# Gated mix of segmented linear-memory attention and a ReGLU feed-forward: value visits in pairs, a ring of eleven exponential tiles, and a new written-out order

## The chip, the cores and the metric

The kernel runs on one core of one Trainium2 chip. Its time is the device time of one execution in microseconds (us), lower is better; three runs of the kernel before have a median of 267.24 us. Engines are named as in the profile: PE is TensorE (matmuls; PEld its weight loads), DVE is VectorE, ACT is ScalarE, POOL is GpSimd, SP is SyncE, which here issues DMAs.

## The reference

Input is x of 2048 tokens by 512. The output is g * a + (1 - g) * b with a gate g per token, an attention branch a and a feed-forward branch b. Cut to what is computed:

```python
g = sigmoid((x * gate_w).sum(-1))                    # per token
# attention branch: 32 heads of 16, 4 segments of 512 tokens
for s in range(4):
    p     = softmax(q_s @ k_s.T / 4 + causal_mask)   # within the segment
    a_dot = p @ v_s
    a_mem = (phi(q_s) @ M) / (phi(q_s) @ z + 1e-6)   # phi(t) = t + 1 if t > 0 else exp(t)
    o_s   = gb * a_mem + (1 - gb) * a_dot            # gb = sigmoid(beta), per head
    M, z  = M + phi(k_s).T @ v_s, z + phi(k_s).sum()
a = concat(o_s) @ wo
# feed-forward branch
b = (relu(x @ W_gate) * (x @ W_up)) @ W_down         # 512 -> 1792 -> 512
```

## The kernel before

Everything stays in SBUF after the first loads. The work is cut into four segments of 512 tokens, and in each segment into four units c of 128 channels, which are eight heads. Units are counted through: segment 0 has units 0 to 3, segment 3 has 12 to 15 in that count of sixteen, and a unit pair is two units that follow each other.

Each piece of work is a step with a name, a list of steps it comes after, and one function that emits its instructions (`Plan.add`, L123). The order is not searched for when the kernel is built: `ORDER` (L41 to L100) is a list of numbers, each one a step and the engine that runs it, and `lay_out` (L137) only puts the steps into their engines' queues in that order and hands out PSUM banks. So which engine evicts what, and what stands behind what on each queue (SP's too), is written out by hand. Every engine runs its queue strictly in order.

PSUM has eight banks. Four are one tile, `sp` (L241), for logits. The other four are `rb` (L242); a step that needs one takes it, and the step that reads it out gives it back.

The kinds of visit to TensorE that the change and the prediction speak of:

- *Ordinary visits* use the whole array: projections Q and K (L477) and V (L519; L502 in segment 0), gate and up (L894), down (L928) and the output projection (L941), retrievals from the memory (MR, L678). Each takes one `rb` bank. Evictions are on ScalarE or VectorE (L373 and L375; L906 and L908 for relu; L913 for the product).
- *Logits visits* (QK, L735) fill `sp`. They work on eight small tiles of the array at once, 4 x 2. Even heads use K itself, odd heads a copy in which the even heads' rows are zero (KTo, made by L490 or L492). Nine logits visits serve a unit pair. Each is followed by one exponential of 128 x 2048 on ScalarE (L746) into one of the E tiles, which form a ring of NE, and by masks on GpSimd (L756), one for each 64-row half of a diagonal block. There is one `sp`, so a logits visit waits for the exponential of the one before.
- *Value visits* (PV, L783), one for a unit, multiply the eight groups of a unit's E tiles with V. They work on tiles 2 x 4 and take two `rb` banks. Each bank is read by a transpose on VectorE (L801) into one of two tA tiles, and then by a chain of three operations (L806, L809, L812); the next transpose into the same tA tile waits for the chain's end. A transpose back (L828) and the memory's part (L834) follow.
- *Memory visits* (MZ, L632) work on tiles 1 x 4, one for a segment but the last.

The key blocks of a unit are packed into E tiles by `BINS`: a unit has eight blocks of 64 keys, block ck with 512 - 64 ck columns of queries. Tiles 0 to 3 of a pair hold the first unit's blocks as `BINS` lists them, tile 4 holds block 4 of both units, tiles 5 to 8 the second unit's.

```python
BINS = ((0,), (1, 7), (2, 6), (3, 5))                                  # L30
parts[w].append((5 * w + b, w, L - 64 * ck, ck, 64 * ck, at))          # L717
a = add(f"QK{seg}{c0}{f}", {"PE": 0.262}, qk, mode="rows", ... fills[-1:] ...)   # L739
b = add(f"EX{seg}{c0}{f}", {"ACT": 1.773}, ex,                         # L747
        after=[a] + readers.get(n - NE, []) + ([masks[n - NE]] if n >= NE else []), ...)
pp = a = add(f"PV{seg}{c}", {"PE": 1.02}, pv, mode="cols2",            # L788
             after=[masks[base + f] for f in need] + d["V"] + d["VS"], take=2, ...)
```

KTo and the tile of phi(Q) (pqT, L555, read by the retrievals) are there twice, one for even and one for odd segments.

In the order before, a value visit stands between ordinary and logits visits, one by one: the first unit's some way into its pair's nine logits visits or behind them, the second unit's later.

## Time and profile before

| what | value |
|---|---|
| median of three runs | 267.24 us (266.77 to 267.49) |
| span of the profiled execution | 265.0 us |
| logits visits, exponentials | 72, 135.1 us of ScalarE |
| masks | 256, 112.3 us of GpSimd |
| value visits | 16 |
| HBM read and written | 8.26 MB and 2.10 MB |

The profile gives the span of one execution, from its first instruction to its last; no time around the span is known for that execution, so it stands beside the median of the runs, which is 2.2 us above it. In rows of a group, after the bar, stand busy time in us, mean ns of one, and the idle time of the engine just before them with what ended most of it. In rows of the timeline stand start in us, duration in us, engine, line and operation. The durations of matmuls are modelled and overlap, so the starts are what is read. In rows of waits stand the waiting engine, tile and line, what it waited for, and then us in total, times and the longest.

### The profile page before, as it was taken

Reading aid. Unit: us, or ns where it says so; the run is one execution under the profiler, and the core shown is the slowest. Engines: PE = TensorE matmul, PEld = TensorE weight load, DVE = VectorE, ACT = ScalarE, POOL = GpSimd, SP = SyncE. Lnnn points to the kernel's source line nnn. Section 1 sums busy time; section 2 is a strip of 40 time slices with the busy share of each in tenths; the row PEclk is TensorE's granted clock in tenths of the full one; section 3 lists DMA queues with packets and bytes.
Section 4 is the critical chain, followed back from the end, with each engine's and each line's share of the span. In section 5 each row is a group of like instructions: output and inputs, shape, how many; then the busy total and the mean of one; then the engine's idle time right before and its main releaser. Section 6 shows DMA issues by size and latency. Waiting matters only on the chain.

```text
span 265.0 us, 7943 instructions
## 1 busy us (share of the span) xinstructions
PE 258.1 (97%) x3293; PEld 121.0 (46%) x3337; DVE 181.0 (68%) x449; ACT 189.7 (72%) x185; POOL 143.7 (54%) x328
## 2 busy tenths in 40 slices
PE   7999999999999999999999999999999999999995
PEld 5444443545444444434444445454544444444554
DVE  1589788897774538855896476688878367666911
ACT  3699799987868786887777686886766576767012
POOL 8038978782826641378758464366468156064010
DMA  6978680426501000030403110000023100031002
GB/s 197 314 166 264 149 288 3 71 74 89 79 4 37 25 2 2 20 82 1 104 2 82 25 42 2 0 4 2 2 61 87 42 20 2 0 81 23 0 2 79
DMA packets 33422, 16.77 MB, mean 63 GB/s; under 512 B 20074, under 2 KB 33386, under 8 KB 33386
## 3 DMA queue, kind: packets, MB, share of 16 engines
q1 hardware_dynamic: 33098, 16.00, 24.3%
q8 instruction: 26, 0.43, 0.7%
q10 hardware_dynamic: 288, 0.26, 0.3%
q14 instruction: 10, 0.08, 0.1%
HBM read 8.26 MB, written 2.10 MB: 39 GB/s over the span
## 4 chain that ended last, share of the span: by engine, by line
PE 94%; DMA 1%; DVE 1%; issue 1%; ACT 1%; SPq 0%
PE rb L894 36%; PE rb L928 17%; PE rb L477 11%; PE sp L735 9%; PE rb L783 7%; PE rb L941 5%; PE rb L519 4%; DMA wv_sb<-in_A_wv_dram 1%; PE rb L678 1%; PE rb L852 1%; PE rb L502 1%; DVE hT L913 1%; ACT E L746 1%; PE rb L632 1%; PE rb L860 0%
## 5 line engine op out<-in xcount | busy, mean ns | idle before, releaser
L746 ACT ACTIVATE E<-sp 128x2048 bf16<-128x2048 f32 x72 | 135.1, 1877 | 35.0 <-PE sp L735 32.8
L756 POOL TENSOR_SCALAR_AFFINE_SELECT E<-E 64x256 bf16<-64x256 bf16 x256 | 112.3, 438 | 82.2 <-ACT E L746 68.7
L894 PE MATMUL rb<-xT,wg_sb 128*128 128x512 bf16 x216 | 55.4, 380 | 0.4
L894 PE MATMUL rb<-xT,wu_sb 128*128 128x512 bf16 x208 | 54.9, 380 | 0.8
L913 DVE TENSOR_TENSOR hT<-rb,rg 128x512 bf16<-128x512 f32 x56 | 38.2, 686 | 20.1 <-PE rb L894 14.1
L928 PE MATMUL rb<-wd_sb,hT 128*128 128x512 bf16 x198 | 48.6, 380 | 0.8 <-issue 0.2
L894 PEld LDWEIGHTS <-wg_sb 128*128 128x128 bf16 x224 | 20.7, 98 | 24.8 <-issue 3.1
L894 PEld LDWEIGHTS <-wu_sb 128*128 128x128 bf16 x224 | 20.1, 98 | 23.5 <-issue 4.5
L735 PE MATMUL sp<-QT,KT 16*64 16x320 bf16 (+7 forms) x512 | 30.3, 295 | 0.0
L735 PE MATMUL sp<-QT,KTo 32*64 32x320 bf16 (+7 forms) x512 | 30.3, 295 | 0.0
L928 PEld LDWEIGHTS <-hT 128*128 128x128 bf16 x210 | 19.4, 98 | 23.8 <-issue 3.2
L801 DVE STREAM_TRANSPOSE tA<-rb 128x512 f32<-128x512 f32 x32 | 21.9, 700 | 12.0 <-PE rb L783 11.6
L906 ACT ACTIVATE rg<-rb 128x512 bf16<-128x512 f32 x36 | 21.3, 598 | 10.1 <-PE rb L894 7.1
L735 PEld LDWEIGHTS <-KT 16*64 16x64 bf16 x512 | 10.5, 102 | 27.5 <-issue 26.9
L908 DVE TENSOR_SCALAR rg<-rb 128x512 bf16<-128x512 f32 x20 | 13.8, 688 | 7.5 <-PE rb L894 7.3
L783 PE MATMUL rb<-E,Vs 64*32 64x448 bf16 (+7 forms) x512 | 18.8, 284 | 0.0
L783 PE MATMUL rb<-E,Vp 64*32 64x448 bf16 (+7 forms) x512 | 18.4, 284 | 0.0
L950 ACT ACTIVATE osb<-rb,ngcol 128x512 bf16<-128x512 f32 x8 | 5.5, 691 | 16.2 <-PE rb L941 16.2
L952 DVE TENSOR_SCALAR osb<-rb,ngcol 128x512 bf16<-128x512 f32 x7 | 5.2, 750 | 16.1 <-PE rb L941 15.9
L477 PE MATMUL rb<-xT,wq_sb 128*128 128x512 bf16 x63 | 16.1, 380 | 0.0
L812 DVE TENSOR_TENSOR o<-tA,co 128x256 bf16<-128x256 f32 x32 | 15.4, 493 | 0.2
L477 PE MATMUL rb<-xT,wk_sb 128*128 128x512 bf16 x59 | 15.4, 379 | 0.2
(97 smaller groups left out, 298.3 us busy)
## 6 DMA issues: line engine op xcount, KB each, us to landing
out_dram<-osb SPq DMA_DIRECT2D x15, 128.0 KB, 1.8
wd_sb<-in_B_W_down_dram SPq DMA_DIRECT2D x1, 1792.0 KB
wg_sb<-in_B_W_gate_dram SPq DMA_DIRECT2D x3, 512.0 KB, 6.3
wu_sb<-in_B_W_up_dram SPq DMA_DIRECT2D x3, 512.0 KB, 6.0
Vs<-Vp SPq DMA_DIRECT2D x8, 144.0 KB, 3.2
wk_sb<-in_A_wk_dram SPq DMA_DIRECT2D x2, 256.0 KB, 3.9
wq_sb<-in_A_wq_dram SPq DMA_DIRECT2D x2, 256.0 KB, 4.7
wo_sb<-in_A_wo_dram SPq DMA_DIRECT2D x1, 512.0 KB, 4.2
```

The source lines that it names most:

```text
L477: nc.tensor.matmul(rb[s.bank][:], lhsT=w[:, ci, c * P:(c + 1) * P], rhs=xT[i][:, ci, :], start=(ci == 0), stop=(ci == NC - 1))
L735: nc.tensor.matmul(sp[64 * h:64 * h + 64, j, off:off + m], lhsT=kt[32 * j:hi, c0 + w, 64 * ck:64 * ck + 64], rhs=QT[i][32 * j:hi, c0 + w, ...
L746: nc.scalar.activation(Er[n % NE][:], sp[:], ACT.Exp, scale=SCALE)
L756: nc.gpsimd.affine_select(out=v, in_=v, compare_op=ALU.is_ge, fill=0.0, base=0, pattern=[[0, 4], [1, 64]], channel_multiplier=-1)
L783: nc.tensor.matmul(rb[s.banks[h]][32 * j:32 * j + 32, q0:q0 + m], lhsT=v[64 * h:64 * h + 64, ck // 2, o:o + 32], rhs=Er[(base + f) % NE][6 ...
L801: nc.vector.transpose(tA[k].rearrange("p b w -> p (b w)"), rb[a.banks[r]][:])
L812: nc.vector.tensor_tensor(o16[u % 2][:, :, r, :], tA[k][:, :, 0:DH], cos[k][:, :, None].to_broadcast([P, NB, DH]), ALU.mult)
L894: nc.tensor.matmul(rb[s.bank][:], lhsT=w[:, ci, fv * P:(fv + 1) * P], rhs=xT[i][:, ci, :], start=(ci == 0), stop=(ci == NC - 1))
L906: nc.scalar.activation(rgb[k][:], rb[a.bank][:], ACT.Relu)
L908: nc.vector.tensor_scalar(rgb[k][:], rb[a.bank][:], 0.0, None, ALU.max)
L913: nc.vector.tensor_tensor(hT[:, fv, :], rb[a.bank][:], rgb[k][:], ALU.mult)
L928: nc.tensor.matmul(rb[b][:], lhsT=hT[:, fv, lc:lc + P], rhs=wd_sb[:, fv, :], start=(fv == 0), stop=False)
```

## The change

- Both value visits of a unit pair stand back to back on TensorE, between two logits visits or behind the last ordinary visit.
- The ring of E tiles has eleven instead of nine.
- KTo and pqT are there once; the KTo mask of a segment now also comes after the logits visits of the segment before, and phi(Q) after the retrievals of the segment before (until now, of the one before that).
- `BINS` puts block 0, the one with 512 columns and two masks, into the last tile of each unit and not into the first.
- `ORDER` is written anew for all engines: other places of steps, and other engines for some of those that two engines can run.

```diff
-NE = 9
+NE = 11
-BINS = ((0,), (1, 7), (2, 6), (3, 5))
+BINS = ((1, 7), (2, 6), (3, 5), (0,))
 ORDER = [
...
-    KTo = [sb([NC, L], BF16, f"KTo{i}") for i in range(2)]
-    pqT = [sb([NC, L], BF16, f"pqT{i}") for i in range(2)]
+    KTo = sb([NC, L], BF16, "KTo")
+    pqT = sb([NC, L], BF16, "pqT")
...
-            d["KO"].append(add(f"KO{seg}{c}", {"DVE": 0.27, "ACT": (0.62, 60.0)}, ko, after=[d["K"][c]], prio=want))
+            d["KO"].append(add(f"KO{seg}{c}", {"DVE": 0.27, "ACT": (0.62, 60.0)}, ko,
+                               after=[d["K"][c]] + (st[seg - 1]["qk"][c] if seg else []), prio=want))
...
                 d["PQ"].append(add(f"PQ{seg}{c}", {"DVE": dve(L)}, pq2,
-                                   after=[m] + (old["mr"] if old else []), prio=want))
+                                   after=[m] + st[seg - 1]["mr"], prio=want))
...
-                        kt = KTo[i] if h else KT[i]
+                        kt = KTo if h else KT[i]
```

The order on TensorE around the first value visits, by the steps' names (U, G gate and up, V, K, Q projections, D down; first digit the segment), before:

```
QK007 | V121 U0_3 | PV00 | QK008 | V130 G0_6 K13 G0_7 | QK020 ...
QK022 | MZ0 | G0_9 | PV01 | QK023 | V120 G0_13 U0_9 MR11 | QK024
```

and after:

```
QK008 | G0_8 Q12 U0_6 | QK020 | K13 G0_10 U0_10 | QK021 | PV00 PV01 | QK022 | V120 G0_11 G0_13 | QK023
```

Behind the pairs stand, in the new order: units 0-1, 2-3, 6-7 and 10-11 a logits visit; units 4-5, 12-13 and 14-15 a gate or up visit; units 8-9 a memory visit.

## The prediction

> **What bounds the kernel now.** I read the page's busy table and its chain first, then TensorE's own waits, then TensorE's timeline where it goes from one kind of work to another.

> ```profile
> span 265.0 us, 7943 instructions
> PE 258.1 (97%) x3293; PEld 121.0 (46%) x3337; DVE 181.0 (68%) x449; ACT 189.7 (72%) x185; POOL 143.7 (54%) x328
> ...
> PE 94%; DMA 1%; DVE 1%; issue 1%; ACT 1%; SPq 0%
> ```

> TensorE is busy 97% of the span and carries 94% of the chain that ended last. A busy TensorE is no proof that it never waits, since matmul ends are modelled. So the next view is what TensorE waited for:

> ```profile
> PE rb L380 <- DVE zeros L252: 1.0, 1, 1.0
> PE rb L502 <- DMA wv_sb<-in_A_wv_dram: 0.3, 1, 0.3
> PE rb L390 <- DMA xT<-in_A_x_dram: 0.3, 1, 0.3
> PE rb L928 <- issue: 0.2, 1, 0.2
> ```

> Except for 0.2 us these waits belong to the first loads. Between them and the end the next matmul always stands ready. So the time is the sum of what TensorE streams plus what it pays for changing its tiling. No other engine has anything to give unless it makes TensorE wait. The price of a change stands in the starts of the timeline:

> ```profile
> 41.25 1.03 PE L894 MATMUL rb<-xT,wg_sb 128*128 128x512 bf16 x4
> 42.11 1.03 PE L894 MATMUL rb<-xT,wu_sb 128*128 128x512 bf16 x4
> 43.07 0.21 PE L735 MATMUL sp<-QT,KT 16*64 16x64 bf16 x1
> ...
> 43.12 0.35 PE L735 MATMUL sp<-QT,KT 16*64 16x448 bf16 x1
> ...
> 43.43 0.82 PE L894 MATMUL rb<-xT,wu_sb 128*128 128x512 bf16 x3
> ```

> An ordinary visit of four matmuls follows its like after 42.11 - 41.25 = 0.86 us. The one ahead of a logits visit takes 43.07 - 42.11 = 0.96, so the change to another tiling costs 0.10. The logits visit lasts 43.43 - 43.07 = 0.36 with its own change back. A value visit:

> ```profile
> 88.30 0.21 PE L783 MATMUL rb<-E,Vs 64*32 64x64 bf16 x4
> ...
> 88.90 0.56 PE L783 MATMUL rb<-E,Vp 64*32 64x448 bf16 x8
> 89.09 0.39 PE L783 MATMUL rb<-E,Vs 64*32 64x512 bf16 x4
> ...
> 89.40 0.24 PE L735 MATMUL sp<-QT,KT 16*64 16x128 bf16 x1
> ```

> It lasts 1.10 us. Inside it, the group of 448 columns passes to the next group after 0.19 us, so the last one, of 512, would pass to another group of the same tiling after 0.19 x 512/448 = 0.22. It passes to the logits visit after 0.31, so leaving the tiling costs about 0.09 to 0.10.

> **The change, part by part.** I counted the tiling changes in the two orders of TensorE's instructions: 164 before, 151 after.

> *Entries.* An ordinary visit stands ahead of a visit of another tiling 73 times before (63 logits, 8 value, 2 memory) and 68 times after (67 logits, 1 value). 5 x 0.10 = 0.5 us saved.

> *Pairs.* Eight value visits now run straight into the second of their pair. 8 x 0.10 = 0.8 us saved. That same-tiling visits join without a price is seen only between the groups of one visit, never between two visits; the term lies between 0 and 8 x 0.12 = 1.0 (0.31 less 0.19, the price if the last group passed as fast as the one ahead of it). I take 0.8 because groups of one visit already go to a different E tile each.
> [...]

> *The same matmuls.* Streams, shapes and counts are unchanged: a logits visit has 512 columns for each of its tiles whether it holds one part or two, so the new bins move no time on TensorE.

> *The first loads.* The order changes before the first logits visit:

> ```profile
> 4.36 1.04 PE L502 MATMUL rb<-wv_sb,xT 128*128 128x512 bf16 x4
> 5.66 0.74 PE L502 MATMUL rb<-wv_sb,xT 128*128 128x512 bf16 x2 [0.26 <-DMA wv_sb<-in_A_wv_dram]
> 6.36 0.40 PE L390 MATMUL rb<-ident,xT 128*128 128x128 bf16 x4
> ```

> ```profile
> L894 PE MATMUL rb<-xT,wg_sb 128*128 128x512 bf16 x216 | 55.4, 380 | 0.4
> ```

> Before, four matmuls run from 4.36, and then TensorE waits for a piece of wv. After, one of those four stands behind the two at 5.66. Those two last 0.74 together and a matmul of this size 0.38, so the second starts at 6.02 and has streamed its 0.22 (0.86 / 4) by 6.24; 0.12 was idle ahead of the transposes at 6.36. A matmul of 0.22 put there loses 0.1 us: at most 0.22, at least 0 if the transposes behind it wait for a copy anyway.

> *The logits loop.* There is one sp tile, so each logits visit waits for the exponential before it.

> ```profile
> 57.81 0.21 PE L735 MATMUL sp<-QT,KT 16*64 16x64 bf16 x1
> ...
> 60.44 0.24 PE L735 MATMUL sp<-QT,KT 16*64 16x128 bf16 x1
> ...
> 63.05 0.27 PE L735 MATMUL sp<-QT,KT 16*64 16x192 bf16 x1
> ```

> ```profile
> 58.31 1.88 ACT L746 ACTIVATE E<-sp 128x2048 bf16<-128x2048 f32 x1
> ...
> 61.00 1.88 ACT L746 ACTIVATE E<-sp 128x2048 bf16<-128x2048 f32 x1
> ```

> From visit to exponential 0.50 and 0.56, the exponential 1.88, and the next visit 0.25 and 0.17 after its end. TensorE did not stall there, so the loop can be as short as 0.50 + 1.88 = 2.38, and is certainly served at 2.61. Counting visits in the new order at the prices above, 17 of the 71 distances between logits visits are 2.65 or less (11 before). Two of them hold nothing but the pair between two logits visits (units 0-1 and 10-11): 0.36 + 1.00 + 1.10 = 2.46. Each may stall 0 to 0.15. The others stand at 2.55 or 2.61, like those that ran freely before. Cost 0 to 0.3, I take 0.1.

> *The banks.* A value visit takes two of the four rb banks, so a pair takes all four, and every ordinary visit behind a pair waits for a transpose on VectorE to give one back.

> ```profile
> 89.54 1.31 DVE L801 STREAM_TRANSPOSE tA<-rb 128x512 f32<-128x512 f32 x2 [2.59 <-PE rb L783]
> ```

> ```profile
> L801 DVE STREAM_TRANSPOSE tA<-rb 128x512 f32<-128x512 f32 x32 | 21.9, 700 | 12.0 <-PE rb L783 11.6 <-ACT e1k L608 0.3
> L812 DVE TENSOR_TENSOR o<-tA,co 128x256 bf16<-128x256 f32 x32 | 15.4, 493 | 0.2
> L806 DVE RECIPROCAL co<-tA 128x16 f32<-128x16 f32 x32 | 7.0, 231 | 0.1
> L809 DVE TENSOR_TENSOR co<-co,Gs 128x16 f32<-128x16 f32 x32 | 6.7, 213 | 0.1
> ```

> ```profile
> L906 ACT ACTIVATE rg<-rb 128x512 bf16<-128x512 f32 x36 | 21.3, 598 | 10.1 <-PE rb L894 7.1 <-DVE hT L913 1.5 <-DVE co L809 0.7
> L908 DVE TENSOR_SCALAR rg<-rb 128x512 bf16<-128x512 f32 x20 | 13.8, 688 | 7.5 <-PE rb L894 7.3
> ```

> Counted from the first visit's start: its transposes start at 89.54 - 88.30 = 1.24, give the first bank back at 1.94 and the second at 2.55. The pair ends at 1.00 + 1.10 = 2.10. Where a logits visit follows (four pairs) the first bank is back in time. In the other four an ordinary or memory visit comes at 2.10 with 0.16 to spare, and a semaphore must still be passed: 0 to 0.1 each, I take 0.1 for all. Ahead of a pair, the second visit needs the last ordinary visit's bank, which has 1.00 of first visit and mostly a logits visit in front of it; an eviction takes 0.60 us on ScalarE or 0.69 on VectorE (the two rows above), so it is hidden; if ScalarE stood in an exponential (1.88) instead, that pair would lose about 0.8.

> ```profile
> L756 POOL TENSOR_SCALAR_AFFINE_SELECT E<-E 64x256 bf16<-64x256 bf16 x256 | 112.3, 438 | 82.2 <-ACT E L746 68.7
> ```

> *What lies beside TensorE and costs nothing unless it becomes late.* Single KTo and phi(Q) tiles make the KTo mask wait for the logits visits of the segment before, and phi(Q) for its retrievals. Behind the waiting instruction stand evictions on VectorE or ScalarE. In the new order each such mask stands well behind the visits it waits for, and the segment's first logits visit comes later still. Eleven E tiles instead of nine let exactly two tiles of the next unit pair be filled before the pair must have read; the pair stands right there (behind the first or second logits visit of the next pair), so the exponential of the third has nothing to wait for. The masks keep their number (256, row above); the last tile's go from four to two, so they end 2 x 0.44 = 0.9 us sooner, and only the last group of a pair, 0.8 + 1.0 us from its start, reads that tile.

> Operations change engines: ScalarE gives seven evictions of about 0.60 to VectorE (0.69) and takes one KTo mask; VectorE gives GpSimd three smaller operations net and takes over one memory-state write. VectorE is idle for 84 us of the span, so only the place of each matters (the banks, above). On SP two loads of 512 KB pass ahead of the second segment's x transposition, whose first reader stands behind the fifth logits visit and not, as before, behind the third. The third segment's transposition is the narrow one:

> ```profile
> 60.80 1.04 PE L894 MATMUL rb<-xT,wu_sb 128*128 128x512 bf16 x3
> ...
> 67.93 0.59 PE L477 MATMUL rb<-xT,wk_sb 128*128 128x512 bf16 x2
> ```

> ```profile
> xT<-in_A_x_dram SPq DMA_TRANSPOSE x3, 4.8
> ```

> The last reader of the old x starts 7.1 us ahead of the first of the new one. In the new order five visits of 0.86, three of half that and three logits visits of 0.46 with their entry lie between: 7.0. The reader itself takes 1.0 and the landing 4.8, so about 1 us is spare.

> ```profile
> 261.65 0.39 PE L860 MATMUL rb<-wo_sb,oT 128*128 128x128 bf16 x4
> ```

> *The end* keeps its last visit, evictions and store, so the 3.4 us from the last visit (261.65) to the span's end stay.

> **Sum.** -0.5 - 0.8 + 0.1 + 0.1 + 0.1 = -1.0 us: the profiled span of 265.0 becomes 264.0, and the median of 267.24, which lies 2.2 above the span, becomes **266.2**.

> The rivals need one row more, of busy time in a stretch (its length, then PE, PEld, DVE, ACT and POOL, the granted clock, DMA share and GB/s):

> ```profile
> 35.20:61.70 26.50, 26.18 (x419) 12.49 (x424) 23.14 (x55) 24.49 (x28) 20.23 (x45) 1.00 0.38 104
> ```

> **Rivals.** (1) *The gain is eaten by small waits.* A pair makes TensorE need four banks and the exponential at set moments; the 17 short loops and eight pairs each losing some 0.05 to 0.1 more make 0.5 to 0.8: 266.9, within 0.3%. For it: in this stretch VectorE (23.1 of 26.5) and ScalarE (24.5) are nearly full already, and in the new order seven short loops follow each other there. Against: TensorE did not wait in that stretch before.

> (2) *The joint saves nothing* because the second visit's weights or banks are not ready: only the entries are left, -0.5 + 0.3 = -0.2: 267.0.

> (3) *Slower: banks come back too late.* There are two tA tiles, so the pair's third transpose waits for the first chain: 2.55 + 0.23 + 0.21 + 0.49 + 0.70 = 4.18 from the pair's start. The third ordinary visit behind a pair comes at about 4.3, with bank three or the first visit's bank (last matmul at 2.75, eviction from 3.2 to 3.9). This decides as soon as VectorE has one eviction of 0.69 in front of the third transpose and the first bank's eviction behind it: then about 0.45 us is lost at each such pair, in six pairs 2.7, and the time is 266.2 + 2.7 = 268.9. For it: VectorE gets more evictions. Against: ScalarE can take the first ones, and the order can be laid so.
> [...]

> **How the numbers follow.** Forecast 0.56; rival 1 0.26; rival 2 0.07; rival 3 0.11. The likeliest case alone spans 265.7 (every stall zero, 1.0 for the joints) to 266.5. Rivals 1 and 2 reach 267.4; leaving out most of rival 3 and a little on the fast side gives 265.6 to 267.4. A change of 0.3%, 0.8 us, is about what a measurement of this kernel can tell from none, so faster means below 266.44: the forecast and a little of rival 1, 0.57; within 0.3% the rest of rivals 1 and 2, 0.31; slower 0.12.

> **What would show it.** In the changed profile the last group (512) of a pair's first visit should pass on after 0.22 and not 0.31, so that this visit lasts 1.00. TensorE's waits should still list only the first loads, or small ones on L801 behind pairs and L746 in the two short loops. The prediction is wrong if TensorE waits in mid-run on VectorE (rival 3), on a mask, or on the x transposition, or if the start loses more than 0.2.

## The result, and the profile after

The changed kernel takes **275.02 us** (median of six runs, 272.6 to 277.4) where the kernel before takes 267.18 in the same session: 1.028 times as long, interval 1.025 to 1.030. It is 2.8% slower; the ratio leaves out the run of 277.4, whose granted clock was lower than that of the other five (0.988 against 0.993 to 1.000). The prediction said 266.2 us, 265.6 to 267.4, and gave slower a chance of 0.12. It was wrong.

The page of the changed kernel (its profiled execution took 274.39 us): span and TensorE's busy time, the granted clock in 40 slices, the queue that brings TensorE's instructions, and the chain that ended last.

```profile
span 272.7 us, 7949 instructions
...
PE 260.6 (96%) x3296; PEld 124.0 (45%) x3337; DVE 184.9 (68%) x457; ACT 187.4 (69%) x179; POOL 148.8 (55%) x326
...
PEclk9999999799999999999999999999999999999999
...
q8 instruction: 26, 0.43, 0.7%
...
PE 95%; issue 3%; DMA 1%; DVE 0%; DVEq 0%
```

The span grew by 7.7 us, TensorE's busy time by only 2.5, and "issue" (time in which TensorE waited for nothing that the profile shows) rose from 1% to 3% of the chain. In one slice the granted clock falls to 0.7; before it was full throughout. TensorE's waits name the places:

```profile
PE rb L786 <- issue: 2.0, 2, 1.1
PE sp L738 <- issue: 1.7, 1, 1.7
PE rb L635 <- issue: 1.4, 1, 1.4
PE rb L382 <- DVE zeros L254: 1.0, 1, 1.0
```

L786 is the value visit, L738 the logits visit, L635 the memory visit. None of the waits that the prediction feared is there: no bank, no exponential, no mask, no transposition. TensorE's timeline around the first pair (the same matmuls as in the kernel before, three lines further down in the code):

```profile
43.05 0.21 PE L786 MATMUL rb<-E,Vs 64*32 64x64 bf16 x4
...
43.83 0.40 PE L786 MATMUL rb<-E,Vs 64*32 64x512 bf16 x8
44.05 0.24 PE L786 MATMUL rb<-E,Vp 64*32 64x64 bf16 x8
...
45.23 0.27 PE L738 MATMUL sp<-QT,KT 16*64 16x192 bf16 x1
47.18 0.24 PE L738 MATMUL sp<-QT,KTo 32*64 32x192 bf16 x1 [1.69 <-issue]
...
49.04 2.52 PE L897 MATMUL rb<-xT,wg_sb 128*128 128x512 bf16 x6 [0.22 <-issue]
```

The joint is as forecast: the group of 512 passes on after 44.05 - 43.83 = 0.22, and the pair's first visit lasts 1.00. But then TensorE does the first matmul of the logits visit and stands still for 1.95 us before the second. Shortly behind it, six matmuls fill the time from 49.04 to 51.49, 0.41 us each where 0.215 is usual (0.86 for four), with the granted clock at 0.5. Busy time by stretches (the granted clock is the third number from the end):

```profile
44.00:48.00 4.00, 2.31 (x94) 1.42 (x77) 1.81 (x6) 1.40 (x2) 3.11 (x5) 0.97 0.22 77
48.00:52.00 4.00, 3.78 (x19) 1.46 (x19) 2.72 (x6) 2.16 (x3) 1.64 (x4) 0.60 0.02 4
```

The trace's clock record has 0.5 from 47.76 to 51.17 us, 3.41 us in all. There are four more such stalls: 1.35 us inside PV03 (at 70.48), 1.3 inside PV13 (131.4), 1.6 ahead of the last matmul of the memory visit MZ2 (163.7) and 0.36 inside PV23 (197.2). These are distances between the starts of matmuls; the weight loads stand still up to 0.2 us longer.

**What the five places share.** I numbered TensorE's own instructions (each matmul is a weight load and a multiply; the page has 3337 and 3296 of them, so 41 multiplies have no record in this trace and were counted by their weight loads). The stalls stand at numbers 961, 1729, 3265, 4289 and 5057: each is 193 more than a multiple of 256. TensorE's list has some 6,680 instructions, and the page's instruction queue brought 0.43 MB in 26 packets of 16,384 B: 64 B an instruction, 256 instructions a packet. The trace dates the packets. For each stall, from the moment when TensorE passed the place 193 modulo 256 ahead of it (by the starts of the weight loads):

| stall in | packet starts | it takes | the 256 instructions had run after | TensorE goes on after | from the packet's end |
|---|---|---|---|---|---|
| QK022 | +1.59 us | 1.00 | 2.18 us | 4.14 us | 1.55 |
| PV03 | +0.97 | 0.97 | 1.79 | 3.33 | 1.39 |
| PV13 | +0.48 | 0.97 | 1.60 | 2.92 | 1.47 |
| MZ2 | +1.15 | 0.96 | 1.86 | 3.59 | 1.48 |
| PV23 | -0.34 | 1.15 | 1.91 | 2.36 | 1.55 |

The fourth and fifth columns give the stall: 4.14 - 2.18 = 1.96, and so on. A pair is 2 x 64 matmuls, 256 instructions in 2.2 us; with a memory visit (128 instructions in 0.6 us) or logits visits (32 in 0.3) beside it there are over 300 in one quick run. In the kernel before the quickest block of 256, counted from one place 193 modulo 256 to the next, took 3.65 us.

### The profile page after: what moved, and what is told of

The parts are those of the page before. It is cut to its first block, busy times and chain, and to the rows that moved or that the text cites. A ratio compares the mean times of both kernels' runs of the same rounds, so it can differ in the third digit from the quotient of the medians.

```text
span 272.7 us, 7949 instructions
## 1 busy us (share of the span) xinstructions
PE 260.6 (96%) x3296; PEld 124.0 (45%) x3337; DVE 184.9 (68%) x457; ACT 187.4 (69%) x179; POOL 148.8 (55%) x326
## 4 chain that ended last, share of the span: by engine, by line
PE 95%; issue 3%; DMA 1%; DVE 0%; DVEq 0%
PE rb L897 37%; PE rb L931 17%; PE rb L479 10%; PE sp L738 9%; PE rb L786 7%; PE rb L944 5%; PE rb L522 4%; PE rb L505 2%; PE rb L681 1%; PE rb L855 1%; DMA xT<-in_A_x_dram 1%; PE rb L635 1%; PE rb L392 1%; PE rb L863 0%; DVE rg L874 0%
## 5 line engine op out<-in xcount | busy, mean ns | idle before, releaser
L759 POOL TENSOR_SCALAR_AFFINE_SELECT E<-E 64x256 bf16<-64x256 bf16 x256 | 113.5, 443 | 100.0 <-ACT E L749 88.3
L897 PE MATMUL rb<-xT,wg_sb 128*128 128x512 bf16 x214 | 56.2, 387 | 0.7 <-issue 0.2
L738 PE MATMUL sp<-QT,KTo 32*64 32x512 bf16 (+7 forms) x512 | 30.3, 295 | 1.7 <-issue 1.7
L738 PE MATMUL sp<-QT,KT 16*64 16x512 bf16 (+7 forms) x512 | 30.6, 295 | 0.0
L909 ACT ACTIVATE rg<-rb 128x512 bf16<-128x512 f32 x34 | 20.0, 596 | 10.7 <-PE rb L897 5.9
L804 DVE STREAM_TRANSPOSE tA<-rb 128x512 f32<-128x512 f32 x32 | 21.2, 693 | 7.5 <-PE rb L786 7.3
L738 PEld LDWEIGHTS <-KT 16*64 16x64 bf16 x512 | 10.6, 102 | 31.4 <-issue 30.5
L911 DVE TENSOR_SCALAR rg<-rb 128x512 bf16<-128x512 f32 x22 | 15.1, 686 | 8.0 <-PE rb L897 6.9
L786 PE MATMUL rb<-E,Vs 64*32 64x448 bf16 (+7 forms) x512 | 18.6, 284 | 1.0 <-issue 1.0
L786 PE MATMUL rb<-E,Vp 64*32 64x448 bf16 (+7 forms) x512 | 17.9, 284 | 1.1 <-issue 1.1
L944 PE MATMUL rb<-wo_sb,oT 128*128 128x512 bf16 x57 | 14.5, 380 | 0.2
L522 PE MATMUL rb<-wv_sb,xT 128*128 128x256 bf16 (+1 forms) x96 | 14.5, 277 | 0.1
L955 DVE TENSOR_SCALAR osb<-rb,ngcol 128x512 bf16<-128x512 f32 x8 | 6.0, 750 | 12.6 <-PE rb L944 12.6
```

The costliest lines, as they stand in the source:

```text
L522: nc.tensor.matmul(rb[s.bank][:, 0:n], lhsT=xT[i][:, ci, t * P:(t + 1) * P], rhs=wv_sb[:, ci, h * D // 2:h * D // 2 + n], start=(ci == 0), ...
L738: nc.tensor.matmul(sp[64 * h:64 * h + 64, j, off:off + m], lhsT=kt[32 * j:hi, c0 + w, 64 * ck:64 * ck + 64], rhs=QT[i][32 * j:hi, c0 + w, ...
L759: nc.gpsimd.affine_select(out=v, in_=v, compare_op=ALU.is_ge, fill=0.0, base=0, pattern=[[0, 4], [1, 64]], channel_multiplier=-1)
L786: nc.tensor.matmul(rb[s.banks[h]][32 * j:32 * j + 32, q0:q0 + m], lhsT=v[64 * h:64 * h + 64, ck // 2, o:o + 32], rhs=Er[(base + f) % NE][6 ...
L804: nc.vector.transpose(tA[k].rearrange("p b w -> p (b w)"), rb[a.banks[r]][:])
L897: nc.tensor.matmul(rb[s.bank][:], lhsT=w[:, ci, fv * P:(fv + 1) * P], rhs=xT[i][:, ci, :], start=(ci == 0), stop=(ci == NC - 1))
```

## The experiments

**Theory A**: TensorE runs out of instructions. In the table it goes on with a new block of 256 only 2.36 to 4.14 us after it passed the place 256 ahead; where the 256 in between run in 1.60 to 2.18 us, it stands. **Theory B**: the banks come back late (rival 3 of the prediction), **theory C**: the exponential tiles or sp hold it up, both hidden behind the word "issue". Theories B and C tie the stalls to the pair, theory A to the number in the list.

**1. Shift the numbers, keep the work.** 81 tiny matmuls behind the warm-up.

```diff
+            for k in range(81):
+                h, j = k // 4 % 2, k % 4
+                nc.tensor.matmul(rb[2 + h][32 * j:32 * j + 32, 0:8], lhsT=zeros[64 * h:64 * h + 64, 0:32],
+                                 rhs=zeros[64 * h:64 * h + 64, 0:8], start=True, stop=True,
+                                 tile_position=(64 * h, 32 * j), skip_group_check=True)
```

> The changed kernel with 81 tiny matmuls on zeros (64x32 tiles, 8 columns: 162 instructions of TensorE) behind the warm-up; nothing else is touched, and the tiny matmuls write regions that later work overwrites. Theory A (TensorE runs out of instructions): its list comes in blocks of 16,384 B (26 packets on the instruction queue for some 6,700 instructions, so 256 instructions of 64 B in each), and all five mid-run stalls of the changed kernel stand at places 193 modulo 256 of that list, where 256 instructions had run in 1.65 to 2.2 us. The shift moves every place by 162, so the stalls in the visits 01 to QK022, 03 to QK101, 21 to MZ2 and 23 to QK302 go, and one of about 1.9 us stands in PV13 at 128 to 131 us, which now holds a place 193 modulo 256 at the end of a full block of value matmuls. Half clock as after the 1.95 us stall may follow that one. Time 268 to 270 us: 266.2 with the forecast's saving, 1.9 for the one stall, up to 1.7 for half clock, and about 0.5 for the tiny matmuls at the start. Theory B (banks come back late from VectorE's transposes) and theory C (the exponential tiles or sp hold TensorE up in the pairs): the visits, their data and their neighbours are as they were, so the stalls keep their places in the steps, and the time is 274.5 to 276 us. Theory D (chance of the clock): 272 to 277 us, with no tie to a place in the list.

Measured 270.83 us, 1.013 times before (1.010 to 1.016): 4.2 us faster than the changed kernel by adding work. Four of the five stalls are gone, the granted clock of the profiled execution is full (of the other three, two had a mean of 0.994 and took 271.0 and 271.4), and one stall is left, at the forecast place. It is larger (2.85 us from matmul to matmul), and the start costs 0.6 us; so the time lies above the 268 to 270 expected. The waits and the timeline of this run:

```profile
PE rb L791 <- POOL E L764: 2.5, 1, 2.5
PE sp L743 <- ACT E L754: 0.2, 1, 0.2
PE rb L686 <- DVE mtok L706: 0.2, 1, 0.2
```

```profile
128.35 0.39 PE L791 MATMUL rb<-E,Vp 64*32 64x448 bf16 x4
131.23 0.40 PE L791 MATMUL rb<-E,Vp 64*32 64x512 bf16 x4 [2.50 <-POOL E L764]
```

Here the profile names a releaser, a mask on GpSimd, and it is a coincidence. GpSimd's four masks ran as one group from 129.96 for 2.18 us. In the changed kernel the same masks and the same last group of PV13 stand so:

```profile
133.32 2.18 POOL L759 TENSOR_SCALAR_AFFINE_SELECT E<-E 64x256 bf16<-64x256 bf16 x4
```

```profile
133.42 0.39 PE L786 MATMUL rb<-E,Vs 64*32 64x512 bf16 x4
```

There the group ran 0.1 us after the first of these masks had begun, so it doesn't need them. The last number ahead of the gap in the shifted run is again 193 modulo 256.

**2. Shift the other way, by 16.**

```diff
-NWARM = 19
+NWARM = 11
-                nc.tensor.matmul(rb[3][:, 0:P], lhsT=zeros[:], rhs=zeros[:], start=True, stop=True)
+                nc.tensor.matmul(rb[3][:, 0:224], lhsT=zeros[:], rhs=gin[:, 0:1].to_broadcast([P, 224]), start=True, stop=True)
```

> The changed kernel with a warm-up of 11 matmuls of 224 columns in place of 19 of 128: as long, but 16 instructions fewer ahead of everything, so every place in TensorE's list moves back by 16. Theory A: places 193 modulo 256 of the list move 16 instructions later in the work; stalls stand at some six or seven places, 16 instructions further on than in the changed kernel or newly at the pairs 10 to 11 and 12 to 13, together 7 to 10 us, time 275 to 279 us. Theories B and C: the same five stalls at the same matmuls, 274 to 276 us. Told apart by the matmul at which each stall stands rather than by the time.

Measured 284.4 us. The time can't be used as it stands: the warm-up now reads gin and waited for its load, which moved the first logits visit from 13.41 to 21.99 us. Without those 8.6 us it is 275.8, within theory A's 275 to 279 and just inside the 274 to 276 of the other two. The places decide:

```profile
PE rb L382 <- DMA gin<-in_gate_w_dram: 10.5, 1, 10.5
PE sp L738 <- issue: 4.2, 3, 1.8
PE rb L786 <- issue: 2.3, 2, 1.2
```

```profile
53.83 0.27 PE L738 MATMUL sp<-QT,KTo 32*64 32x192 bf16 x1
53.91 0.29 PE L738 MATMUL sp<-QT,KT 16*64 16x320 bf16 x1
55.61 0.32 PE L738 MATMUL sp<-QT,KTo 32*64 32x320 bf16 x1 [1.41 <-issue]
```

In QK022 the stall stood behind the first matmul; now it stands behind the ninth, eight matmuls or 16 instructions further on. The one of MZ2 moved on into QK222, the one of PV03 into QK101, and the pair PV10 PV11, which had none, has one of 1.56. Every one that the trace shows stands at the same place modulo 256. In QK022 the tiles that the stalled matmul reads, QT and KTo, had already served four matmuls of the same visit. That the stall moved by exactly the 16 instructions taken away ahead of it speaks against a wait for data.

**3 and 4. Half as many instructions for the same streaming**, in the changed kernel and, as a control, in the kernel before.

```diff
-                    for h, j in ((h, j) for h in range(2) for j in range(4)):
+                    for h, j in ((h, j) for h in range(2) for j in (0, 2)):
...
-                        nc.tensor.matmul(rb[s.banks[h]][32 * j:32 * j + 32, q0:q0 + m],
-                                         lhsT=v[64 * h:64 * h + 64, ck // 2, o:o + 32],
+                        nc.tensor.matmul(rb[s.banks[h]][32 * j:32 * j + 64, q0:q0 + m],
+                                         lhsT=v[64 * h:64 * h + 64, ck // 2, o:o + 64],
```

> The changed kernel with half as many value matmuls, each on a 64x64 tile in place of two on 64x32 tiles: two heads share one matmul on the exponentials of the first, so a value visit issues 64 instructions and not 128, and its output is not that of the reference (half of the heads get the weights of their neighbour; the rest of the work is unchanged). The columns that a row and column group streams stay as they were, so a visit should last about as long. Theory A: 256 instructions now take no less than some 3 us anywhere, no stall is left, no half clock, time 265.5 to 267 us, and 0.5 to 1.2 us below the kernel before with the same halving. Theories B and C: TensorE reaches the logits visits, the banks and the tiles as early as before, so the stalls of 6.8 us stay, 273 to 276 us. If a 64x64 tile costs more or less by itself, that shows in the kernel before with the same edit.

> The kernel before with the same halving of its value matmuls (64x64 tiles, half of the heads with the weights of their neighbour, so not the reference's output): the control for the run on the changed kernel. All theories: no stall stood in the kernel before, so 266.5 to 267.8 us if a 64x64 tile streams like two 64x32 tiles side by side; the difference between the two halved kernels is the worth of the order without the stalls, forecast as 1.0 us in favour of the changed order by theory A and 6 to 9 us against it by theories B and C.

Measured 266.11 us for the changed order (0.996 of before, 0.994 to 0.997) and 267.25 for the order before (1.000, 0.999 to 1.001). The same pairs, banks, tiles and neighbours, and no stall is left in the list of waits. TensorE's waits in the halved changed kernel:

```profile
PE rb L382 <- DVE zeros L254: 1.0, 1, 1.0
PE rb L505 <- DMA wv_sb<-in_A_wv_dram: 0.2, 1, 0.2
```

A remainder of 0.2 us is left inside PV03, where a whole block of 256 still passes in 2.5 us: a group of 448 columns there passes on after 0.40 instead of 0.19, 1.50 us after the end of a packet, and the pair takes 2.32 us where the other seven take 2.09 or 2.10. So the expectation that no 256 would run in less than some 3 us was wrong at this place, and by the time from the packet's end the delay there is of the same kind as the five.

This run also prices each stall, since nearly everything else keeps its rhythm (the stall in PV03 comes out 0.2 too small, for the reason just given). Starts of logits visits in the two timelines:

| visit | changed | halved | lag | what came in between |
|---|---|---|---|---|
| QK022 | 45.23 | 44.59 | 0.64 | the start (0.54 at the first logits visit) |
| QK023 | 51.49 | 47.22 | 4.27 | stall 1.95, half clock 1.68 |
| QK101 | 72.15 | 66.88 | 5.27 | stall in PV03 |
| QK201 | 133.74 | 127.13 | 6.61 | stall in PV13 |
| QK222 | 165.41 | 157.19 | 8.22 | stall in MZ2 |
| QK302 | 197.93 | 189.58 | 8.35 | stall in PV23 |
| end | 272.68 | 264.14 | 8.54 | |

From the stall's end to QK023 the changed kernel takes 51.49 - 47.18 = 4.31 us, the halved one 47.22 - 44.59 = 2.63 for the whole visit: 1.68 goes to the halved clock.

**5. Undo one pair.** Shifted by 162, with PV13 taken away from PV12 (behind QK202). Here and in experiment 8 TensorE's part of the order is shown by the steps' names.

```diff
-NWARM = 19
+NWARM = 13
+            for k in range(87):
...
 ORDER = [
...
-QK200 MZ1 PV12 PV13 QK201 D11 K23 QK202
+QK200 MZ1 PV12 QK201 D11 K23 QK202 PV13
```

> The changed kernel with its places in TensorE's list moved by 162 instructions (13 warm-up matmuls and 87 tiny ones on zeros, where there were 19 warm-up matmuls) and one pair undone: the value visit PV13, where the run with the shift alone still stalled by 2.85 us, goes behind QK202 instead of directly behind PV12. Seven pairs stay. Theory A (instructions come in blocks of 256, and two blocks may not follow each other within about 3.8 us): no stall of over 0.3 us is left, no half clock, time 265.8 to 266.9 us, 0.1 to 0.2 us above the changed order with halved instructions (266.1 us), which makes it faster than the kernel before by 0.1 to 0.5%. If pairs or banks were the cause, the seven pairs left would keep most of the stalls, and the time would stand at 271 us or above.

Measured 269.0 us, 1.009 times before (1.006 to 1.011). The mid-run stalls are gone with seven pairs kept, but the time lies 2.1 us above the upper end of what I expected. The waits, in us, without "issue" in mid-run:

```profile
PE rb L877 <- DVE tA L750: 0.3, 1, 0.3
PE sp L684 <- ACT E L695: 0.3, 1, 0.3
PE rb L627 <- DVE mtok L647: 0.2, 1, 0.2
```

L877 is a down visit that waits for a bank from VectorE's transpose: moving one value visit by hand, with the other engines' order left as it was, brings back the wait of rival 3, and PV13's new place costs 0.9 us (the lag behind the halved kernel grows from 1.89 at QK200 to 2.81 at QK203). The wait on mtok stands ahead of the move, at 84.87. The start is 0.9 us later than in the changed kernel (first logits visit 14.28).

**6. Quick instructions without pairs.** The kernel before, 64 tiny matmuls ahead of each value visit.

```diff
             def pv(e, s, c=c, base=base):
+                for k in range(64):
+                    h, j = k // 4 % 2, k % 4
+                    nc.tensor.matmul(rb[s.banks[h]][32 * j:32 * j + 32, 448:456], ...
```

> The kernel before, in its own order with single value visits, with 64 tiny matmuls on zeros (64x32 tiles, 8 columns: 128 instructions) ahead of each of the 16 value visits; they write a stretch of the visit's own banks that the visit then overwrites. Theory A: 256 instructions now pass in about 1.5 us around each visit, so where a block of 256 ends there TensorE runs out; stalls at places 193 modulo 256 of the list, 1 to 2.3 us each, at two to five of the 16 visits, 3 to 7 us in all, on top of 16 times about 0.35 us for the tiny matmuls themselves: 275 to 280 us. If the pairs, the banks or the exponential tiles were the cause, nothing but the tiny matmuls is added: 272 to 274 us and no such stalls.

Measured 276.7 us, inside theory A's range, but not for its reason. The tiny matmuls cost about 0.55 us a visit and not 0.35 (16 x 0.55 = 8.8 of the 9.7), and only one stall came, of 0.6 us:

```profile
194.15 0.64 PE L781 MATMUL rb<-zeros 64*32 64x8 bf16 x64
194.62 0.22 PE L788 MATMUL rb<-E,Vs 64*32 64x64 bf16 x4
...
195.48 0.40 PE L788 MATMUL rb<-E,Vs 64*32 64x512 bf16 x4
196.48 1.89 PE L899 MATMUL rb<-xT,wg_sb 128*128 128x512 bf16 x8 [0.60 <-issue]
```

It stands at 192 or 193 modulo 256, so a stall of this kind needs no pair; but a quick block alone does not make one either. Blocks that ran in 1.3 to 1.7 us passed freely where their packet had started 0.5 to 1.9 us before TensorE reached the place, that is, where slow 128x128 matmuls stood just ahead of it. The pair PV10 PV11 of the changed kernel, quick but without a stall, had its packet 1.69 us ahead too. The same holds for blocks of 2.3 to 2.7 us in experiments 1, 5 and 8, with packets 0.8 to 1.3 us ahead; the expectation of experiment 5, that two blocks may not follow each other within about 3.8 us, is too strict. The packets of the five stalls in the table started from 0.34 us ahead to 1.59 us behind. What sets this lead was not tested by itself; my count of two to five stalls was too high because I gave the lead too little.

**7. The supply alone.** 2048 quick instructions in a row behind the warm-up.

```diff
+            for k in range(1024):
+                h, j = k // 4 % 2, k % 4
+                nc.tensor.matmul(rb[2 + h][32 * j:32 * j + 32, 0:8], ...
```

> The kernel before with 1024 tiny matmuls on zeros (64x32 tiles, 8 columns: 2048 instructions, eight blocks of 256) behind the warm-up. It measures the supply of instructions by itself, with nothing else for TensorE to wait on. Theory A: TensorE stands still once in every 256 instructions at places 193 modulo 256, and the blocks follow each other at an even pace of 2.0 to 3.9 us where the 256 instructions run in about 0.9 us, so the burst takes 16 to 31 us. If instructions are always there in time, the burst takes 2048 times about 3.5 ns, 7 us, with no gaps.

Measured: 28.8 us for the burst (first logits visit at 42.85 instead of 14.01), inside theory A's 16 to 31. Waits between 3 and 32 us, and the timeline:

```profile
PE rb L383 <- issue: 19.3, 7, 3.4
```

```profile
8.45 1.18 PE L383 MATMUL rb<-zeros 64*32 64x8 bf16 x128 [3.45 <-issue]
13.00 1.18 PE L383 MATMUL rb<-zeros 64*32 64x8 bf16 x128 [3.37 <-issue]
17.00 1.18 PE L383 MATMUL rb<-zeros 64*32 64x8 bf16 x128 [2.82 <-issue]
20.45 1.18 PE L383 MATMUL rb<-zeros 64*32 64x8 bf16 x128 [2.27 <-issue]
24.18 1.18 PE L383 MATMUL rb<-zeros 64*32 64x8 bf16 x128 [2.55 <-issue]
27.91 1.18 PE L383 MATMUL rb<-zeros 64*32 64x8 bf16 x128 [2.55 <-issue]
```

128 matmuls, 256 instructions, run in 1.18 us, and then TensorE waits for the next block: one block every 3.45 to 3.73 us from 17 us on, and 4.0 to 4.55 before that, while the first loads keep the DMA engines 70 to 96% busy. That is the price by itself, with no data to wait for.

**8 and 9. All pairs kept, the numbers chosen.** 92 tiny matmuls ahead of 16 warm-up matmuls, and MZ1 moved from between QK200 and PV12 to behind QK128; the control is the kernel before with the same start.

```diff
-NWARM = 19
+NWARM = 16
+            for k in range(92):
...
 ORDER = [
...
-QK128 U1_12 U1_13 U1_11 QK200 MZ1 PV12 PV13 QK201
+QK128 MZ1 U1_12 U1_13 U1_11 QK200 PV12 PV13 QK201
```

> The changed kernel with all eight pairs kept and nothing left out of the work; its places in TensorE's list are moved by 178 instructions (92 tiny matmuls on zeros ahead of 16 warm-up matmuls, where there were 19), and MZ1 (64 matmuls, 128 instructions), which stood ahead of PV12 and PV13, goes behind QK128. Theory A: no two blocks of 256 instructions follow each other too fast any more, so no stall of over 0.2 us in mid-run and no half clock; 266.3 to 267.5 us, being the 266.1 of the changed order with halved instructions and 0.2 to 1.2 for the tiny matmuls at the start and what they shift. If pairs, banks or the exponential tiles caused the stalls, they are all still there: 271 us or more.

> The kernel before with the same start as the run with all pairs kept (92 tiny matmuls ahead of 16 warm-up matmuls): the control for it. All theories: no mid-run stall, 267.0 to 268.3 us, being the kernel before and 0 to 1.2 us of the start. Theory A has the changed order 0.5 to 1.1 us below this one; if the order itself is no gain without the stalls, the two agree within 0.3 us.

Measured 267.99 us (1.004 of before, 1.002 to 1.006) and 267.85 for the control (1.004, 1.002 to 1.005). With all eight pairs and all of the work, 7.0 of the 7.8 us are back; theories B and C had 271 or more. Against its control the order brings nothing, though: 0.1 us slower, where I expected 0.5 to 1.1 faster. The profiled execution of the order with all pairs is the slowest of its eleven (270.03 us, with the first logits visit 1.1 us later than in the control's), so its trace can be read for places and waits but not for the time. Its waits in mid-run:

```profile
PE rb L877 <- issue: 0.3, 2, 0.2
PE rb L877 <- DVE tA L750: 0.3, 1, 0.3
PE rb L627 <- DVE mtok L647: 0.2, 1, 0.2
```

No version tried here beats the kernel before with the full work.

## Why the prediction was wrong, point by point

**What bounds the kernel** failed, in one sentence: "So the time is the sum of what TensorE streams plus what it pays for changing its tiling." There is a third term, the supply of instructions, which stood at zero in the kernel before because no block of 256, as the packets cut the list, ran in less than 3.65 us. That may have been luck in part: from 46.5 us the kernel before runs 256 instructions (MZ0, a gate visit and most of PV01) in 2.18 us, but a place 193 modulo 256 falls inside that run. The row of the instruction queue was on the page before as well, with its 26 packets; I read it as traffic and never asked how fast TensorE eats a packet. "*The same matmuls.* Streams, shapes and counts are unchanged" is true, and was the wrong thing to count: what changed is how close together they stand.

The traces show the blocks (26 packets of 16,384 B, stalls at one place modulo 256) and their price: in the burst 256 instructions were executed in 1.18 us, and from 17 us on a block came every 3.45 to 3.73.

**Pairs, -0.8.** The joint itself was right: 1.00 for the first visit, 0.22 for its last group. The term was not, for it took the second visit to be as long as before. But in these runs 128 quick instructions right behind 128 quick ones are no longer free inside the second visit. Its group of 192 columns passes on after 0.15, in the changed kernel's pair PV10 PV11 (first fence), and after 0.08 with half the instructions (second):

```profile
101.22 0.21 PE L786 MATMUL rb<-E,Vs 64*32 64x64 bf16 x4
...
102.31 0.41 PE L786 MATMUL rb<-E,Vp 64*32 64x192 bf16 x8
102.46 0.39 PE L786 MATMUL rb<-E,Vs 64*32 64x256 bf16 x8
...
103.41 0.39 PE L897 MATMUL rb<-xT,wg_sb 128*128 128x512 bf16 x1
```

```profile
96.04 0.22 PE L786 MATMUL rb<-E,Vs 64*64 64x64 bf16 x2
...
97.14 0.35 PE L786 MATMUL rb<-E,Vp 64*64 64x192 bf16 x4
97.22 0.40 PE L786 MATMUL rb<-E,Vs 64*64 64x256 bf16 x4
...
98.13 0.60 PE L897 MATMUL rb<-xT,wg_sb 128*128 128x512 bf16 x2
```

From its start to the next visit the whole pair takes 103.41 - 101.22 = 2.19 us with all instructions and 98.13 - 96.04 = 2.09 with half. All eight pairs of experiment 8 take 2.16 to 2.19; a single visit of the kernel before takes 1.10 to 1.13, two of them 2.20 or a little more. So 0.07 to 0.10 of each 0.10 is given back, and the term is at most 8 x 0.03 = 0.2 or so and not 0.8. Right behind a stall (PV13 of the changed kernel) the same group passed on after 0.09. The hole goes with the number of instructions (0.15 with all, 0.08 with half); what makes it was not shown.

**Entries, -0.5.** An entry still costs what was said: the visit ahead of QK120 starts at 99.91 and the logits visit at 100.86, 0.95 against 0.86. The sum over five fewer of them was not measured by itself.

**The sum of -1.0.** The two halved kernels differ by 267.25 - 266.11 = 1.14 us: with the supply out of the way the forecast was right to 0.2 us (four runs of 265.86 to 266.43 against ten of 266.44 to 267.46). With the full number of instructions the kernel with all pairs and its control differ by 0.1 the other way. What lies between is the hole (8 times 0.07 to 0.10), the waits of 0.2 to 0.3 us on VectorE in the rows above, and MZ1's move; I did not separate them.

**The logits loop, +0.1, and the banks, +0.1.** Nothing of either is in the waits of the changed kernel. The bank wait of 0.3 shows only where I moved a visit myself; behind the first pair of the halved kernel TensorE stands still for 0.14 (47.77) until one of VectorE's transposes ends.

**The first loads, +0.1.** Not settled. The changed kernel and its halved twin have the same order at the start and reach the first logits visit at 13.41 and 12.87, so one execution says no more than 0.5 us there.

**The rivals.** Rival 3 had the right sign and a false reason: VectorE's transposes ended no wait of the changed kernel. Rival 1's small waits did not come in the changed kernel; with most of the stalls gone and the order untouched, experiment 1 shows two of 0.2 us, on an exponential and on VectorE (its rows of waits). Rival 2 ("The joint saves nothing") was nearly right about the size of the joint, 2.16 to 2.19 us a pair against 2.2, but the hole goes with the number of instructions (0.15 against 0.08), and no bank was waited for there. No case in the list had the supply of instructions, so the range had no room for it. By the table of lags the stalls and the half clock make 3.63 + 1.00 + 1.34 + 1.61 + 0.13 = 7.7 of the 8.5 us by which the changed kernel ends behind its halved twin; 0.5 more is the start. "The prediction is wrong if TensorE waits in mid-run on VectorE, on a mask, or on the x transposition" looked in the wrong place; "issue" was the word to watch.

## What to carry to other kernels

Before setting many small matmuls back to back, count the instructions of the run and not only its columns: in these runs TensorE stopped where it went through a whole block of 256, as the packets cut its list, in 1.2 to 2.2 us with nothing slow just ahead, and lost 0.2 us in a block of 2.5. A quick run that a boundary cut in two passed in the kernel before (256 instructions in 2.18 us). A wait put down to "issue" in the middle of a visit, between two matmuls with the same data, was the sign here (1.7 us in QK022); number the engine's instructions, see whether the stalls share a place modulo 256, and shift them all to make sure. Half as many instructions on 64x64 tiles left no such wait in the list (266.11 us), and the start shifted by 178 instructions with MZ1 moved away from its pair left none over 0.2 us (267.99). Choosing the places by padding alone is fragile: 162 instructions more left one stall, of 2.85 us, and 16 fewer moved the stalls on and let one of 1.56 us appear at PV10 PV11.
